# Local attention's two pairs multiplied with V in one step on four row groups, and V of the strided classes loaded in two transfers a batch

## The chip, the cores and the metric

The kernel runs on one core of one Trainium2 chip. Its five engines work at the same time, each through its own list of instructions in order: TensorE (PE; its weight loads are shown as PEld) multiplies matrices into PSUM, VectorE (DVE), ScalarE (ACT) and GpSimd (POOL) work on elements, SyncE (SP) issues the DMAs, which run on 16 DMA engines. The metric is the device time of one execution in microseconds.

## The reference

Eight batches, eight heads, 576 positions, 64 numbers a head. Heads 0 to 3 see the last 32 positions (local), heads 4 to 7 the earlier positions of the same class modulo 32 (strided, 18 positions a class). The attention's output, 512 wide, goes through a gated layer.

```python
mask_local = (rel >= 0) & (rel < stride)          # stride = 32
mask_strided = (rel >= 0) & (pos[None, :] % stride == pos[:, None] % stride)
scores = np.where(masks[None], scores, -1000000000.0)   # scores = q k^T / sqrt(64)
attn = softmax(scores)
x = (attn @ v) as [batch, seq, 512]
...
gate_pre += conv_w[k][None, None, :] * xp[:, k:k + S, :]   # 5 taps, causal
gate = 1.0 / (1.0 + np.exp(-gate_pre))
out = (gate * (x @ w_val)) @ w_out
```

## The kernel before

The program works on one batch after the other and keeps everything with channels on the 128 partitions, x transposed. A batch has these steps; the letters name them in the whole text.

- L (three a batch): local scores of two pairs of heads, 24 matmuls of 64 x 64 from `qLs` and `KL` into two banks of PSUM; mask by DVE, softmax by DVE, POOL and ACT, then a transpose into `PL`.
- Y (two a batch before): the weights in `PL` times V in `vLs`. `vLs` holds, on the 32 partitions 64a + 32p, half a of the sequence of pair p. One Y takes one pair p: ten key windows, two heads, two halves, 40 matmuls on two row groups (32 partitions each) into two banks. ACT copies each bank into `xs`.
- S (two a batch): strided scores, 32 matmuls from `qSs` and `KBS` into one bank; softmax; transpose into `PT`, copied into a block diagonal `BDS`.
- T (two a batch, each in two halves of 8 matmuls): `vSs` times `BDS` into one bank a half, copied into `xs`.
- X: each 128 channels of `xs` split into a high and a low part (`xhi`, `xlo`). G: the convolution and the gate; one of 32 runs as matmuls on TensorE (the "convolution" of the text, batch 0), the others on DVE.
- V: x times w_val, 12 matmuls of 384 columns for 128 channels, times the gate on DVE, split again (`ghi`, `glo`). P: times w_out, 12 matmuls of 512 columns, copied by ACT into `osb` and stored. V and P run over 12 blocks of 384 rows that go across the batches: 48 V and 36 P.

Every fp32 matmul (L, Y, S, T, convolution) shows in the trace as two passes, each with a weight load; V and P matmuls are one pass each. So one Y of 40 matmuls is 80 rows of the trace.

All q, k and v tiles exist once. A batch's load into `qSs` and `KBS` (four transfers, 1152 KB) must wait until both S steps of the batch before have read them, one into `qLs` and `KL` (1152 KB) for the last L, one into `vLs` (608 KB) for Y and one into `vSs` (576 KB) for T. Transfers stand in one queue, SP's, in a fixed order, and every one also waits for the eighth before it.

What sets the order: each step is put down with `plan.add` (engine, estimated time, group, calls). `Plan.issue` (L133 to L234) then plays the steps on a model of the engines and lets each engine take, of the steps that are ready, the one whose group stands lowest in the list `RANK`; `plan.bank()` gives a step a free bank of the six. Only the order that comes out is in the program. Where the model sees TensorE wait before 75 us, it puts in filler matmuls on a tile `idle` (L351 in the trace, L353 after the change). The trace shows every other step at L226, so steps are told apart by their tiles.

`PAIRS` (L707) says which pairs go into one Y (L532 to L546), `PVL` is the estimate for it, `load` (L301) the estimate for a transfer, `load_v` (L465) issues the loads of V. The layout of `vS` in DRAM is [batch, 4 groups, 18, 8, 256]; group g goes to partitions 32g to 32g + 31, its positions 0 to 15 to every second of them, positions 16 and 17 to two odd ones.

Of the kernel before, what the change touches and what calls it, by code (L numbers as in the profile page):

```python
# [19 lines left out]
NT = 18  # L20
# [3 lines left out]
P = 128  # L24
# [9 lines left out]
class Bank:  # L34
# [12 lines left out]
    def now(self):  # L47
        ap = self.hold["tile"]
        for name, a, k in self.chain:
            ap = getattr(ap, name)(*a, **k)  # L50
        return ap
# [6 lines left out]
class Plan:  # L58
# [11 lines left out]
    ENGINES = ("pe", "dve", "act", "pool", "sp")  # L70
    WINDOW, QUIET, BUSY, SLOW = 3.413, 0.48, 0.85, 1.9

    BLOCK, FETCH = 256, 2.4
    ISSUE, TO_DATA, TO_END = 0.6, 1.2, 0.65

    def __init__(self):
        self.filler, self.banks, self.holds = None, None, []
# [160 lines left out]
def tile_sparse_attention_moe(  # L238
# [13 lines left out]
    nc = tc.nc  # L252
# [6 lines left out]
    plan = Plan()  # L259

    def tiles(n, shape, name, dtype=F32, space=None):
        return [(space or pool).tile(shape, dtype, name=f"{name}{i}") for i in range(n)]
# [10 lines left out]
    def size(ap):  # L273
        n = 1
        for _, k in list(now(ap).ap)[1:]:
            n *= k
        return n
# [17 lines left out]
    def pe(group, took, calls, early=None, part=0):  # L295
        plan.add("pe", took, group, calls, early=early, part=part)

    def mm(out, lhsT, rhs, first=True, last=True):
        return (T.matmul, dict(out=out, lhsT=lhsT, rhs=rhs, start=first, stop=last))

    def load(group, out, in_):  # L301
        n = out.ap[0][1] * size(out)
        plan.add("sp", max(n * 4 / 320e3 + (0.25 if group[-1] == "0" or "w" in group else 0.08), 0.45), group, [(nc.sync.dma_start, dict(out=out, in_=in_))])


    ident = pool.tile([P, P], F32, name="ident")
# [12 lines left out]
    vSs = pool.tile([P, 8, 256], F32, name="vSs")  # L319
# [11 lines left out]
    gates = tiles(4, [P, 2 * S], "gate")  # L331
    BDS = Ring(tiles(NB, [P, 16, 4, NT], "BDS"))
    PS = Ring(tiles(1, [P, 32, 32], "PS"))
# [84 lines left out]
    def weight_part(name, src, dst, e, raw, t, u):  # L418
        raw = raw.rearrange("p (c f) -> p c f", c=4).bitcast(U32)
        load("load " + name, raw, src.bitcast(U32)[:, 2 * P * e:2 * P * (e + 1)].rearrange("(c p) f -> p c f", p=P))  # L420
        cols = slice(P * e, P * (e + 1))
        from_f64("make " + name, raw.rearrange("p c (f w) -> p (c f) w", w=2), t, u, dst[0][:, :, cols], dst[1][:, :, cols])
# [30 lines left out]
    def load_qk(b, kind):  # L453
        group = f"load q{kind}{b}"
        if kind == "L":
            load(group, qLs[:, :, :], qL[b])
            load(group, KL[:, :, STRIDE:], kL[b])
            return

        for j in range(2):  # L460
            load(group, qSs[j::2, :2 * S], qS[b, 64 * j:64 * j + 64])
        for j in range(2):
            load(group, KBS[j::2, j, :, :], kS[b, 64 * j:64 * j + 64])

    def load_v(b, kind):  # L465
        group = f"load v{kind}{b}"
        if kind == "L":

            for a in range(2):
                for p in range(2):  # L470
                    at = slice(64 * a + 32 * p, 64 * a + 32 * p + 32)
                    load(group, vLs[at, 1 - a:], vL[b].rearrange("(w r) f -> r w f", r=32)[:, 8 * a:9 * a + 9, 2 * D * p:2 * D * p + 2 * D])
        else:
            for g in range(4):
                load(group, vSs[32 * g:32 * g + 32:2], vS[b, g, 0:16])
            for g in range(4):
                load(group, vSs[32 * g + 1:32 * g + 32:16], vS[b, g, 16:NT])

    def attend_local(b):
        xs = xss[b % 2]  # L480
# [50 lines left out]

        for ps in PAIRS:  # L532
            group = f"Y{b}.{ps[0]}"
            banks = {(a, p): plan.bank()[:, :HALF] for p in ps for a in range(2)}
            calls = []
            for w in (1, 3, 5, 7, 9, 0, 2, 4, 6, 8):
                for h in range(2):
                    for (a, p), xp in banks.items():
                        rows = slice(64 * a + 32 * p, 64 * a + 32 * p + 32)
                        rhs, q0, n = seen(rows, h, w)  # L540
                        calls.append(mm(xp[64 * h:64 * h + 64, q0:q0 + n], vLs[rows, w, D * h:D * h + D], rhs, w == 1, w == 8))
            pe(group, PVL, calls, early=0.15)
            for p in ps:
# [137 lines left out]
    for b in range(B):  # L681
        load_qk(b, "L")
        load_v(b, "L")
        load_qk(b, "S")
        load_v(b, "S")
        attend_local(b)
        attend_strided(b)
        if b == 0:

            raw = [osb2.rearrange("p i f -> p (i f)"), raws[2], raws[3], osb2.rearrange("p i f -> p (i f)")]  # L690
            for e in range(4):
                weight_part(f"wo{e}", w_out, wo, e, raw[e], *[gates[2 * i + e % 2][:, S:S + DM] for i in range(2)])
            zero("dve", "zero xs1", xss[1][:, :, 0:PADK])
        gate(b)
        for k in ((3 * b // 2,) if b % 2 == 0 else (3 * (b // 2) + 1, 3 * (b // 2) + 2)):
            value(k)
            project(k)
    names = list(dict.fromkeys(s[2] for s in plan.steps))
    tile_sparse_attention_moe.end = plan.issue(dict(zip(names, RANK)))


NB = 1
NPL = 1
TAKEN = set()
WIDE = set()
WIDES = set()
PAIRS = ((0,), (1,))  # L707
PVL = 1.5
CONV = {(0, 0)}
HELD = set()  # L710
RANK = [
# [12 lines left out]
]  # L724


# [39 lines left out]
```

## Time and profile before

| | |
|---|---|
| runs | 331.25, 336.55, 336.93 us; median 336.55 |
| the profiled execution | 331.2 us, span 329.4 us |
| granted TensorE clock, mean | 0.978 |
| TensorE busy | 311.0 us of the span (94%) |
| DVE, ACT, POOL busy | 225.4, 189.8, 180.8 us |
| moved by the DMA queues | 42.98 MB |

A row of the timeline gives the start and the length of a stretch of equal instructions in microseconds, then engine, line, operation, output and inputs, count, and in brackets how long the engine stood idle before it and for what. "issue" is idle time for which the profile shows no cause. Matmuls overlap, so a step's time is read from its start to the start of the step behind it.

### The profile page before, as it was taken

Reading aid. Unit: us, or ns where it says so; the run is one execution under the profiler, and the core shown is the slowest. Engines: PE = TensorE matmul, PEld = TensorE weight load, DVE = VectorE, ACT = ScalarE, POOL = GpSimd, SP = SyncE. Lnnn points to the kernel's source line nnn. Section 1 sums busy time; section 2 is a strip of 40 time slices with the busy share of each in tenths; the row PEclk is TensorE's granted clock in tenths of the full one; section 3 lists DMA queues with packets and bytes.
Section 4 is the critical chain, followed back from the end, with each engine's and each line's share of the span. In section 5 each row is a group of like instructions: output and inputs, shape, how many; then the busy total and the mean of one; then the engine's idle time right before and its main releaser. Section 6 shows DMA issues by size and latency. Waiting matters only on the chain.

```text
span 329.4 us, 11806 instructions
## 1 busy us (share of the span) xinstructions
PE 311.0 (94%) x5113; PEld 261.2 (79%) x5120; DVE 225.4 (68%) x438; ACT 189.8 (58%) x373; POOL 180.8 (55%) x213
## 2 busy tenths in 40 slices
PE   8986999997999999899999998999999989999995
PEld 3545567787889989688998887988998978999884
DVE  4479399997988989698592288876776951764300
ACT  4036675695578746574753294498369748442421
POOL 9664767978653964674384276556067722502610
PEclk9997699999999999999999999999999998999999
DMA  7999944469314452676302476036202200100022
GB/s 236 252 178 329 271 137 154 148 203 258 107 66 146 149 211 100 207 235 176 105 2 84 142 197 211 2 105 175 73 1 66 103 4 32 66 32 32 34 96 96
DMA packets 27267, 42.98 MB, mean 130 GB/s; under 512 B 3088, under 2 KB 16912, under 8 KB 26640
## 3 DMA queue, kind: packets, MB, share of 16 engines
q1 hardware_dynamic: 27216, 42.24, 42.9%
q8 instruction: 40, 0.66, 0.9%
q14 instruction: 11, 0.09, 0.1%
HBM read 32.79 MB, written 9.44 MB: 128 GB/s over the span
## 4 chain that ended last, share of the span: by engine, by line
PE 82%; DMA 10%; issue 3%; SPq 2%; ACT 0%; DVE 0%
PE bank L226 73%; PE bank L351 9%; DMA qSs<-in_qS_dram 6%; DMA vSs<-in_vS_dram 3%; SPq L226 2%; DMA vLs<-in_vL_dram 1%; ACT osb L226 0%; DVE idle L350 0%; DVE none L354 0%
## 5 line engine op out<-in xcount | busy, mean ns | idle before, releaser
L226 DVE SCALAR_TENSOR_TENSOR taps<-xs,cw,taps 128x576 f32<-128x576 f32 x124 | 100.6, 811 | 14.3 <-ACT taps L226 12.5
L226 PE MATMUL bank<-xhi,wv 128*128 128x384 f32 x384 | 99.7, 340 | 0.0
L226 PE MATMUL bank<-wo,ghi 128*128 128x512 f32 x288 | 90.8, 397 | 0.0
L226 POOL TENSOR_TENSOR glo<-GV,ghi 128x384 fp32r<-128x384 f32 x48 | 48.3, 1013 | 63.4 <-ACT ghi L226 62.1
L226 PEld LDWEIGHTS bank<-xhi,wv 128*128 128x128 f32 x384 | 68.8, 188 | 2.2
L226 PE MATMUL bank<-xlo,wv 128*128 128x384 f32 x192 | 64.5, 336 | 0.0
L226 PEld LDWEIGHTS bank<-wo,ghi 128*128 128x128 f32 x288 | 53.6, 190 | 11.2
L226 POOL TENSOR_TENSOR xlo<-xs,xhi 128x576 fp32r<-128x576 f32 x32 | 46.2, 1451 | 19.9 <-ACT xhi L226 19.8
L226 PE MATMUL bank<-wo,glo 128*128 128x512 f32 x144 | 56.5, 393 | 0.0
L226 DVE SCALAR_TENSOR_TENSOR GV<-gate,bank 128x384 f32<-128x384 f32 x48 | 26.0, 547 | 34.1 <-PE bank L226 18.0
L226 ACT ACTIVATE osb<-bank 128x512 f32<-128x512 f32 x36 | 21.2, 596 | 30.0 <-PE bank L226 24.5
L226 ACT COPY xs<-bank 128x288 f32<-128x288 f32 x64 | 32.0, 548 | 8.3 <-PE bank L226 8.1
L226 ACT CAST ghi<-GV 128x384 fp32r<-128x384 f32 x48 | 24.0, 510 | 21.6 <-DVE GV L226 21.4
L226 PEld LDWEIGHTS bank<-xlo,wv 128*128 128x128 f32 x192 | 36.0, 188 | 0.0
L351 PE MATMUL bank<-idle 128*128 128x512 bf16 x117 | 30.5, 411 | 5.2 <-issue 3.8
L226 ACT ACTIVATE gate<-taps 128x576 f32<-128x576 f32 x31 | 20.4, 658 | 24.7 <-DVE taps L226 24.6
L226 ACT COPY BDS<-PT 32x288 f32<-32x288 f32 x64 | 27.7, 433 | 9.7 <-DVE PT L226 8.9
L226 PEld LDWEIGHTS bank<-wo,glo 128*128 128x128 f32 x144 | 27.2, 189 | 5.9
L226 POOL TENSOR_TENSOR SML<-SML,ST 128x384 f32<-128x384 f32 x24 | 20.3, 845 | 19.0 <-DVE ST L226 18.8
L351 PEld LDWEIGHTS <-idle 128*128 128x128 bf16 x124 | 12.2, 103 | 20.6 <-issue 7.8
L226 DVE TENSOR_REDUCE ST<-SML 128x6 f32<-128x384 f32 (+1 forms) x48 | 26.0, 545 | 0.9 <-ACT SML L226 0.5
L226 PEld LDWEIGHTS bank<-PL,vLs 32*64 32x64 f32 x1280 | 21.9, 143 | 5.8 <-issue 3.4
(69 smaller groups left out, 371.1 us busy)
## 6 DMA issues: line engine op xcount, KB each, us to landing
out_dram<-osb SPq DMA_DIRECT2D x36, 256.0 KB
qSs<-in_qS_dram SPq DMA_DIRECT2D x16, 288.0 KB
qLs<-in_qL_dram SPq DMA_DIRECT2D x8, 576.0 KB
KL<-in_kL_dram SPq DMA_DIRECT2D x8, 576.0 KB
KBS<-in_kS_dram SPq DMA_DIRECT2D x16, 288.0 KB
vSs<-in_vS_dram SPq DMA_DIRECT2D x32, 128.0 KB
vLs<-in_vL_dram SPq DMA_DIRECT2D x16, 160.0 KB
vLs<-in_vL_dram SPq DMA_DIRECT2D x16, 144.0 KB
```

The lines of the kernel that those rows point to most:

```text
L226: got = [fn(**{k: now(x) for k, x in kw.items()}) for fn, kw in calls]
L351: plan.filler = lambda at: T.matmul(out=at, lhsT=idle[:, :P], rhs=idle[:, :], start=True, stop=True)
```

## The change

Both pairs' Y become one step: `PAIRS` is one tuple, so four banks are taken, and the inner loop goes over the four (a, p), four row groups in turn. The order of the sums in each bank stays. The eight loads of `vSs` become two, one for positions 0 to 15 of all four groups (64 partitions, 512 KB), one for positions 16 and 17 (8 partitions, 64 KB). The model's figures for transfers, for instruction packets and for Y are set anew, and `RANK` is another list, so all steps stand in another order.

```diff
-    BLOCK, FETCH = 256, 2.4
-    ISSUE, TO_DATA, TO_END = 0.6, 1.2, 0.65
+    BLOCK, FETCH = 256, 3.0
+    ISSUE, TO_DATA, TO_END = 0.6, 1.2, 1.2
...
     def load(group, out, in_):
-        n = out.ap[0][1] * size(out)
-        plan.add("sp", max(n * 4 / 320e3 + (0.25 if group[-1] == "0" or "w" in group else 0.08), 0.45), group, [(nc.sync.dma_start, dict(out=out, in_=in_))])
+        n = 1
+        for k in out.shape:
+            n *= k
+        plan.add("sp", max(n * 4 / 320e3 + LOAD, 0.45), group, [(nc.sync.dma_start, dict(out=out, in_=in_))])
...
-            for g in range(4):
-                load(group, vSs[32 * g:32 * g + 32:2], vS[b, g, 0:16])
-            for g in range(4):
-                load(group, vSs[32 * g + 1:32 * g + 32:16], vS[b, g, 16:NT])
+            for rows, keys in ((slice(0, P, 2), slice(0, 16)), (slice(1, P, 16), slice(16, NT))):
+                load(group, vSs[rows].rearrange("r n f -> r (n f)"),
+                     vS[b, :, keys].rearrange("g t n f -> g t (n f)"))
...
+LOAD = 0.2
-PAIRS = ((0,), (1,))
-PVL = 1.5
+PAIRS = ((0, 1),)
+PVL = 2.2
 RANK = [
-    223, 130, 85, 82, 100, 54, 253, 247, 56, 131, 268, 93, 53, 134, 241, 140, 277, 144, 154, 271, 136, 147, 195, 58,
+    101, 80, 2, 172, 13, 120, 96, 98, 5, 148, 41, 250, 4, 267, 110, 231, 29, 182, 86, 130, 26, 55, 68, 52,
...
```

TensorE at the Y of batch 1 before: the last V matmuls ahead of it and the first of Y (`PL` and `vLs`); the two banks alternate for the first 40 matmuls, then two others do.

```order
L226 MATMUL bank_114<-xhi,wv_85 128x384
L226 MATMUL bank_114<-xhi,wv_86 128x384
L226 MATMUL bank_114<-xlo,wv_85 128x384
L226 MATMUL bank_116<-PL_101,vLs 64x64
L226 MATMUL bank_115<-PL_101,vLs 64x64
```

TensorE at the Y of batch 2 after the change, behind a V as well.

```order
L226 MATMUL bank_116<-xhi,wv_85 128x384
L226 MATMUL bank_116<-xhi,wv_86 128x384
L226 MATMUL bank_116<-xlo,wv_85 128x384
L226 MATMUL bank_113<-PL_101,vLs 64x64
L226 MATMUL bank_117<-PL_101,vLs 64x64
L226 MATMUL bank_115<-PL_101,vLs 64x64
L226 MATMUL bank_114<-PL_101,vLs 64x64
```

Four banks take turns, and the 80 matmuls stand in one run; before they stood in two runs of 40, mostly with other steps between.

SP at the start, before: weights (`w_val`, `w_out`), then q and k, with the loads of `vSs` between.

```order
L226 DMA xs_77<-in_w_val_dram 128x4x256
L226 DMA qSs<-in_qS_dram 64x1152
L226 DMA osb_110<-in_w_out_dram 128x4x256
L226 DMA qLs<-in_qL_dram 128x1152
L226 DMA KL<-in_kL_dram 128x2x576
L226 DMA vSs<-in_vS_dram 16x2048 x2
L226 DMA KBS<-in_kS_dram 64x1152 x2
L226 DMA qSs<-in_qS_dram 64x1152
L226 DMA vSs<-in_vS_dram 16x2048 x2
```

SP after the change, from the sixth transfer of the program to the first load of `vSs`; ahead of it stand two pieces of w_val, conv_w, half of qSs and qLs.

```order
L226 DMA KL<-in_kL_dram 128x2x576
L226 DMA KBS<-in_kS_dram 64x1152
L226 DMA vLs<-in_vL_dram 32x9x128
L226 DMA KBS<-in_kS_dram 64x1152
L226 DMA vLs<-in_vL_dram 32x9x128
L226 DMA vLs<-in_vL_dram 32x10x128 x2
L226 DMA xs_78<-in_w_val_dram 128x4x256
L226 DMA qSs<-in_qS_dram 64x1152
L226 DMA xs_77<-in_w_val_dram 128x4x256
L226 DMA xs_78<-in_w_out_dram 128x4x256
L226 DMA osb_110<-in_w_out_dram 128x4x256
L226 DMA vSs<-in_vS_dram 64x1x2048
```

The second half of qSs went behind all of k, vLs and a third piece of w_val, and the load of vSs behind all of these.

SP after the change where batches 2 and 3 are loaded, for the places where a load of vSs stands between those that S and L wait for.

```order
L226 DMA qSs<-in_qS_dram 64x1152
L226 DMA KBS<-in_kS_dram 64x1152 x2
L226 DMA vSs<-in_vS_dram 64x1x2048
L226 DMA qSs<-in_qS_dram 64x1152
L226 DMA qLs<-in_qL_dram 128x1152
L226 DMA KL<-in_kL_dram 128x2x576
L226 DMA vSs<-in_vS_dram 8x1x2048
```

Before, the same place had four loads of 16x2048 ahead of the first half of qSs and four of 2x2048 ahead of the second.

22 rows, old and new, of the table RANK are left out of this document.

## Prediction

> **What bounds the kernel now.** I read the page first, then the chain of waits, then TensorE's timeline with its idle times. The page:
>
> ```profile
> PE 311.0 (94%) x5113; PEld 261.2 (79%) x5120; DVE 225.4 (68%) x438; ACT 189.8 (58%) x373; POOL 180.8 (55%) x213
> PE   8986999997999999899999998999999989999995
> DMA  7999944469314452676302476036202200100022
> GB/s 236 252 178 329 271 137 154 148 203 258 107 66 146 149 211 100 207 235 176 105 2 84 142 197 211 2 105 175 73 1 66 103 4 32 66 32 32 34 96 96
> q1 hardware_dynamic: 27216, 42.24, 42.9%
> q8 instruction: 40, 0.66, 0.9%
> L351 PE MATMUL bank<-idle 128*128 128x512 bf16 x117 | 30.5, 411 | 5.2 <-issue 3.8
> ```
>
> TensorE is busy 94% of the span and no other engine above 68%. But 117 of its matmuls are fillers (`idle`), 30.5 us, and they stand almost all ahead of the first V step, while the DMA queues run at nine tenths. So there are two stages: up to the first V the kernel waits for loads and for what softmax makes of them; after that TensorE's own work sets the time. The ends of the stages in TensorE's timeline (start, us, operation; idle before it in brackets):
>
> ```profile
> 13.88 1.72 PE L226 MATMUL bank<-KL,qLs 64*32 64x64 f32 x144
> 19.52 0.29 PE L226 MATMUL bank<-KBS,qSs 128*32 128x36 f32 x9
> 20.83 1.26 PE L226 MATMUL bank<-KBS,qSs 128*32 128x36 f32 x119 [1.02 <-issue]
> 27.58 0.82 PE L351 MATMUL bank<-idle 128*128 128x512 bf16 x3 [3.44 <-issue]
> 36.60 3.08 PE L226 MATMUL bank<-xs,gate 128*128 128x288 f32 x8
> 43.37 0.72 PE L226 MATMUL bank<-KL,qLs 64*32 64x64 f32 x48
> 55.83 0.70 PE L226 MATMUL bank<-xhi,wv 128*128 128x384 f32 x2
> ...
> 325.34 0.39 PE L226 MATMUL bank<-wo,glo 128*128 128x512 f32 x1
> ```
>
> The first V starts at 55.8, the last matmul ends at 325.7: 55.8 us and 269.9 us, then 3.7 us to the span's end (329.4) and 1.8 us around it (331.2). In the second stage TensorE stood still only here:
>
> ```profile
> 66.44 0.33 PE L226 MATMUL bank<-KBS,qSs 128*32 128x36 f32 x15 [1.27 <-issue]
> 77.00 1.33 PE L226 MATMUL bank<-KBS,qSs 128*32 128x36 f32 x128 [1.96 <-DMA qSs<-in_qS_dram]
> 138.94 1.33 PE L226 MATMUL bank<-KBS,qSs 128*32 128x36 f32 x128 [1.40 <-DMA qSs<-in_qS_dram]
> 195.63 1.39 PE L226 MATMUL bank<-PL,vLs 32*64 32x64 f32 x78 [0.23 <-DMA vLs<-in_vL_dram]
> 199.35 0.31 PE L226 MATMUL bank<-KL,qLs 64*32 64x64 f32 x7 [1.24 <-issue]
> 224.07 0.46 PE L226 MATMUL bank<-PL,vLs 32*64 32x64 f32 x15 [0.34 <-issue]
> 269.94 0.27 PE L226 MATMUL bank<-PL,vLs 32*64 32x64 f32 x2 [1.00 <-issue]
> 270.39 1.97 PE L226 MATMUL bank<-BDS,vSs 128*64 128x72 f32 x32 [0.18 <-issue]
> ```
>
> Loads 1.96 + 1.40 + 0.23 = 3.6 us, "issue" 4.0 us, together 7.6 us. The "issue" waits all fall in or behind long runs of small matmuls: queue q8 brings 40 packets for some 10,233 matmuls and weight loads (5113 + 5120), 256 instructions each, and a run that goes through them too fast waits for the next packet.
>
> **The Y step in one.** Before, a pair's Y runs 80 passes:
>
> ```profile
> 91.67 0.77 PE L226 MATMUL bank<-KBS,qSs 128*32 128x36 f32 x64
> 92.38 0.74 PE L226 MATMUL bank<-wo,ghi 128*128 128x512 f32 x2
> ...
> 98.08 1.39 PE L226 MATMUL bank<-PL,vLs 32*64 32x64 f32 x80
> 99.41 1.22 PE L226 MATMUL bank<-BDS,vSs 128*64 128x72 f32 x32
> 100.56 0.73 PE L226 MATMUL bank<-KL,qLs 64*32 64x64 f32 x48
> 101.21 0.62 PE L226 MATMUL bank<-xhi,wv 128*128 128x384 f32 x2
> ...
> 103.50 1.39 PE L226 MATMUL bank<-PL,vLs 32*64 32x64 f32 x80
> ```
>
> ```profile
> L226 ACT COPY xs<-bank 128x288 f32<-128x288 f32 x64 | 32.0, 548 | 8.3 <-PE bank L226 8.1
> ```
>
> From the start of one step to the next: Y 1.33 us (two pairs 2.66), T 1.15, L 0.65, V 2.3 with its switch, S 0.71. No row shows four row groups in Y. Bounds for its 160 passes: no more overlap than now, 2.66; the densest stream of the trace, S with 0.71/64 = 11.1 ns a pass, 1.78. L moves 64 columns like Y and takes 0.65/48 = 13.6 ns: 2.2 us. I take 2.2 as the nearest row, a gain of 0.46 us a batch. More than 2.66 I exclude, since the four go to four different banks. Four banks of six are taken at once and cleared by four ACT copies (548 ns each, 2.2 us); a V and a P behind them need two banks, and cover that. If the cover goes, the copies cost up to 2.2 us a batch, which stands in the upper part of the range.
>
> **What the new order does ahead of the first V.** There it now runs nine L steps, not six, and Y of two batches, not one: 3 x 0.65 + 2.66 = 4.6 us of work comes forward into waiting time, and 100 fillers stand there instead of 124. When the first V starts, I follow by the loads. L of batch 0 needs 2484 KB of the SP queue, before 2464: 13.9 as now. S needs the second half of qSs, now behind 4468 KB, before 3584: 884 KB more at about 0.24 MB/us (the first two slices), 3.7 us, so 23.2; the 32 fillers ahead of it, 30.5/117 = 0.26 us each from L's end at 15.6, hold it to 23.9. S 1.4 us, a wait for instructions as now (1.0 to 3.4; I take 2.8), Y 2.2: about 30. The L of batch 1 behind it needs q and k that lie behind 7156 KB: 7.33 MB at 0.24 is 30.5, 32 with landing, if the load of vSs ahead of them is spread evenly. I take 35 (next part). Then two L 1.3, the convolution 6.1 (now 36.60 to 43.37, less one L), L 0.7, half a T 0.6: 43.7. The S of batch 1 waits some 2.3 us for its second half; S 1.4, T 0.6, 11 fillers 2.9, T 1.15, 2 fillers 0.5, three L 2.0, Y 2.2, two waits for instructions 2.3: the first V at 59.0, 3.2 us later than now (54 to 62).
>
> **vSs in two loads.** Four of the eight loads cost the SP queue 2.50 us, and the first load of an S turn is issued at once when the S step of the batch before has ended:
>
> ```profile
> 51.82 2.50 SPq L226 DMA_DIRECT2D vSs<-in_vS_dram  x4
> 68.68 0.51 SPq L226 DMA_DIRECT2D qSs<-in_qS_dram  x1
> ```
>
> Six issues fewer are 6 x 0.63 = 3.8 us of SP a batch. That is on no path of TensorE: it never waited for a vSs load longer than the trace shows above. What changes is how the bytes lie on the sixteen queues. 42.24 MB in 42.9% of 329.4 us is 299 GB/s, 18.7 GB/s a queue. 512 KB over all sixteen take 1.75 us; over four, 7.0 us, and every load issued behind it lands 5.3 us later. No row shows a load of this form: those of before took 16 rows from one run, this one takes 64 rows out of four runs of 16. I choose the four queues, since four is the one count that both the runs and the rows can be dealt by; both ends stay in the range. The Trainium skill says so: in "DMA: Bandwidth & Descriptors", section "Why a DMA increments its semaphore by 16 and not by 1", a DMA uses the largest number of engines up to 16 that divides the slowest dimension of both sides, here 64 and 4; by that rule the sum below holds, by an even spread rival 1 does. No run here shows it yet.
>
> Whom it meets: the S step of batch 2 ended at 68.58 (the V behind it starts there) and the next S could start at 77.00, a turn of 8.4 us for 1152 KB. With the vSs load between them, 13.7.
>
> ```profile
> 68.58 0.61 PE L226 MATMUL bank<-xhi,wv 128*128 128x384 f32 x2
> 317.41 0.61 PE L226 MATMUL bank<-wo,ghi 128*128 128x512 f32 x2
> ...
> 320.13 0.61 PE L226 MATMUL bank<-wo,ghi 128*128 128x512 f32 x2
> ```
>
> A P takes 2.72 us. In the new order stand between one batch's last S and the next one's first: with V at 2.2 in a row: for batch 2 a half T, 13 fillers, T, three L, Y and V, 11.5 us; for batch 3 Y, four V and P, 13.7; for batch 4 T, three V and P, 10.5; later ones 16 and more. So waits of 2.2, 0 and 3.2 us. Batch 7's L loads stand right behind a vSs load that is issued some 3 us before them; of the 5.3 I count another 2: 7.4 us.
>
> **The sum of the second stage.** 269.9; three L gone forward, -2.0; before, seven batches' Y at 2.66, now six at 2.2, -5.4; the old waits -7.6; new waits for loads +7.4; new waits for instructions +2.2 (a Y of 320 instructions in 2.2 us passes one packet's edge; edges less than 3 us apart are left at three places; the old ones came to 4.0): 264.5. With 59.0 ahead and 5.5 behind: 329.0 us against the profiled 331.2, -0.7%.
>
> That execution is like the fastest of the runs (331.25); the other two lie at 336.6 and 336.9, the median at 336.55, 1.6% above it. The trace shows nothing of why, and it may befall the new kernel as well. I say 330 for its median.
>
> **Rivals.** (1) The load is spread evenly. Then the first V stays at 55.8, the load waits shrink to 0.5: 55.8 + 257.6 + 5.5 = 319. 55.8 + 257.6 is 269.9 - 2.0 - 5.4 - 7.6 + 0.5 + 2.2 behind the old start. For it: six issues fewer a batch; against: the four runs. Chance 0.27. (2) Slower: the four queues are slow. At the mean of the first seven slices (222 GB/s, 13.9 a queue) the load takes 9.4 us, 7.1 more than spread. Two such loads ahead of the first V: +3.6. The turn is 15.5: S of batches 2 to 4 wait 4.0, 1.8 and 5.0, +5.4; L of batch 7 waits the whole 7.1, +5.1: 329.0 + 14.1 = 343.1. It decides from a load of about 8 us on. For it: DMA at 9 of 10 all through the start. Against: after 130 us the queues are half idle. Chance 0.18. (3) The change does not do what it says: Y gains nothing from four groups (+0.46 x 6 = 2.8) or loses it to the banks: 332 to 335. Chance 0.10. My forecast keeps 0.45.
>
> **The numbers.** 330; the range from (1) to (2), 319 to 343, leaves a tenth out on each side. A measurement of this kernel tells about 2% from no change. Faster by more: most of (1) and the lower edge of mine, 0.34. Slower by more: most of (2), 0.04 of mine and (3): 0.20. Within: 0.46.
>
> **What would show it.** A Y of 160 passes lasting 2.2 us (1.78 to 2.66) to the next step's start; the first V near 59; waits for qSs or KBS ahead of S of batches 2 and 4; "issue" waits of 2 to 3 us behind the first V. If the DMA share runs at nine tenths while GB/s stays up, and no S waits, rival 1 holds; a first V beyond 62, or waits of 5 us for loads in the later batches, rival 2. I would be wrong altogether if DVE (68%) or ACT became what V and P wait for under the new order.

## The result and the profile after

The changed kernel takes 348.9 us (median of four runs, 347.3 to 353.0); the kernel before, on the same chip, 334.1 (331.3 to 336.9). The ratio is 1.051, with a 95% interval of 1.044 to 1.058: slower. The forecast, 330, and its range, 319 to 343, were wrong. The profiled execution of the changed kernel is the slowest of the four, 353.0 us (span 351.2), so about 4 us of what follows belongs to it alone.

The page after, its lines that answer to those shown of before:

```profile
PE 308.4 (88%) x5096; PEld 258.9 (74%) x5096; DVE 229.0 (65%) x438; ACT 190.0 (54%) x373; POOL 180.7 (51%) x213
PE   8984597689799789799989894996799999999995
PEclk9996589899989999989999998999699999999999
DMA  8998836916625275317820575129300140120022
q1 hardware_dynamic: 26704, 42.23, 44.2%
```

TensorE's busy share fell from 94 to 88%, and no other engine rose to take its place. The dips in its row (slices 4 and 5, 25 and 28) have a lower granted clock in the same slices or the one behind. The same two stages as in the prediction, cut at the start of the first V and at the end of the last matmul, show where the time went. A row gives the stretch, its length, then busy time and instructions of TensorE, its weight loads, DVE, ACT and POOL, then the granted clock, the DMA share and GB/s. Before:

```profile
0.00:55.83 55.83, 48.98 (x904) 28.97 (x912) 37.97 (x85) 26.83 (x54) 37.14 (x55) 0.91 0.87 226
55.83:325.73 269.90, 262.03 (x4211) 232.24 (x4209) 187.41 (x354) 162.37 (x319) 143.67 (x159) 0.99 0.35 112
```

After:

```profile
0.00:64.68 64.68, 49.66 (x1193) 31.03 (x1193) 51.10 (x114) 32.52 (x65) 46.33 (x67) 0.85 0.83 221
64.68:347.46 282.78, 258.70 (x3908) 227.89 (x3904) 177.89 (x324) 156.89 (x307) 134.39 (x147) 0.97 0.37 100
```

The first stage is 8.9 us longer, all but 0.7 of it idle. In the second TensorE has less to do (258.7 against 262.0), but stands still for 24.1 us instead of 7.9. The larger waits, and one Y with the V behind it, in TensorE's timeline after:

```profile
29.64 0.35 PE L226 MATMUL bank<-KBS,qSs 128*32 128x36 f32 x8 [4.87 <-issue]
40.44 0.45 PE L226 MATMUL bank<-KL,qLs 64*32 64x64 f32 x10 [2.85 <-issue]
63.25 1.49 PE L226 MATMUL bank<-PL,vLs 32*64 32x32 f32 x79 [2.28 <-issue]
...
69.33 0.76 PE L226 MATMUL bank<-KBS,qSs 128*32 128x36 f32 x64 [1.56 <-DMA qSs<-in_qS_dram]
82.91 2.09 PE L226 MATMUL bank<-PL,vLs 32*64 32x64 f32 x160
84.92 0.61 PE L226 MATMUL bank<-xhi,wv 128*128 128x384 f32 x2
97.44 1.19 PE L226 MATMUL bank<-KBS,qSs 128*32 128x36 f32 x64 [3.23 <-DMA qSs<-in_qS_dram]
118.92 0.76 PE L226 MATMUL bank<-KBS,qSs 128*32 128x36 f32 x64 [1.95 <-DMA qSs<-in_qS_dram]
147.90 0.95 PE L226 MATMUL bank<-BDS,vSs 128*64 128x72 f32 x16 [1.75 <-ACT osb L226]
177.25 1.22 PE L226 MATMUL bank<-BDS,vSs 128*64 128x72 f32 x32 [1.35 <-DMA vSs<-in_vS_dram]
216.09 0.83 PE L226 MATMUL bank<-KL,qLs 64*32 64x64 f32 x48 [4.59 <-DMA KL<-in_kL_dram]
247.73 1.63 PE L226 MATMUL bank<-KL,qLs 64*32 64x64 f32 x96 [4.67 <-DMA KL<-in_kL_dram]
```

The chain of waits says what these loads stood behind (start, us, what):

```profile
56.63 12.57 DMA qSs<-in_qS_dram
85.34 12.01 DMA qSs<-in_qS_dram
131.40 10.51 DMA out_dram<-osb
196.01 12.40 DMA vSs<-in_vS_dram
208.43 7.53 DMA KL<-in_kL_dram
238.91 10.01 DMA out_dram<-osb
```

The load of vSs issued at 196.01 lands 12.4 us later. Every transfer waits for the eighth before it, and the eighth behind that load, which is for batch 6, is KL of the same batch: SP cannot issue it before 208.43, it lands at 216.0, and L of batch 6 starts at 216.09. L of batch 7 (247.73) waits for a KL that was issued at 235.04, 3.4 us behind a vSs load (231.67). The halves of qSs issued at 56.63 and 85.34, 0.7 and 5.3 us behind a vSs load of 512 KB (at 55.94 and 80.02), take 12 us, and S waits for them (69.33 and 97.44). And two output stores take 10 us: they go through the same queues, `osb` has room for two, so ACT can't clear a P's bank until a store has landed. Both kinds of wait, as SP's own queue and ACT show them after (us, times, longest):

```profile
SPq L226 <- DMA vSs<-in_vS_dram: 23.1, 5, 6.9
...
ACT osb L226 <- DMA out_dram<-osb: 22.6, 6, 6.3
```

Before, SP waited 1.6 us for vSs and ACT 5.3 us for stores.

A wait is also dearer than its length. The stretch around the wait that ends at 247.73, after:

```profile
238.00:243.00 5.00, 5.00 (x174) 3.97 (x172) 4.26 (x10) 3.39 (x8) 3.17 (x5) 1.00 1.02 219
243.00:248.00 5.00, 0.33 (x25) 0.30 (x32) 0.46 (x1) 0.00 (x0) 0.82 (x1) 0.92 0.73 146
248.00:251.40 3.40, 3.17 (x100) 2.60 (x84) 2.69 (x6) 2.44 (x6) 0.74 (x1) 0.50 0.45 144
251.40:255.00 3.60, 3.60 (x12) 2.86 (x11) 2.47 (x7) 3.36 (x7) 2.93 (x4) 0.63 0.14 53
```

Behind 4.67 us of idle time the granted clock is 0.50 for some 6 us, and the P there takes 4.93 us (249.59 to 254.52) instead of the 2.72 of the prediction's row. The Trainium skill has this in "TensorE: Matmul & The Clock Gate", section "HAM oscillation — how this bites in real kernels": gaps of more than about 3.4 us bring the half clock back. The trace agrees for this wait, but gives no such limit: behind the 3.23 us that end at 97.44 the clock is 0.50 as well (to 99.00), behind the 1.75 us that end at 147.90 it is 0.58 (to 150.00), and behind the 1.95 us that end at 118.92 it stays at 1.00. From what length on a wait slows the clock, these runs don't show.

### The profile page after: what moved, and what is told of

Read it like the earlier page. It is cut to its first block, busy times and chain, and to the rows that moved or that the text cites. A ratio compares the mean times of both kernels' runs of the same rounds, so it can differ in the third digit from the quotient of the medians.

```text
span 351.2 us, 11718 instructions
## 1 busy us (share of the span) xinstructions
PE 308.4 (88%) x5096; PEld 258.9 (74%) x5096; DVE 229.0 (65%) x438; ACT 190.0 (54%) x373; POOL 180.7 (51%) x213
## 4 chain that ended last, share of the span: by engine, by line
PE 61%; DMA 31%; issue 2%; ACT 2%; SPq 1%; DVE 1%; ACTq 0%
PE bank L226 56%; DMA qSs<-in_qS_dram 10%; DMA KL<-in_kL_dram 8%; DMA vSs<-in_vS_dram 7%; DMA out_dram<-osb 7%; PE bank L353 5%; SPq L226 1%; ACT osb L226 1%; ACT BDS L226 0%; DVE taps L226 0%; DVE ST L226 0%; ACT gate L226 0%; DVE SML L226 0%; ACT ghi L226 0%; DVE SMS L226 0%
## 5 line engine op out<-in xcount | busy, mean ns | idle before, releaser
L226 PE MATMUL bank<-wo,ghi 128*128 128x512 f32 x288 | 94.8, 411 | 0.2 <-ACT osb L226 0.2
L226 PEld LDWEIGHTS bank<-wo,ghi 128*128 128x128 f32 x288 | 56.1, 199 | 12.6 <-ACT osb L226 0.5
L226 PE MATMUL bank<-wo,glo 128*128 128x512 f32 x144 | 58.2, 404 | 0.0
L226 PEld LDWEIGHTS bank<-wo,glo 128*128 128x128 f32 x144 | 28.2, 196 | 6.4
L226 PE MATMUL bank<-KL,qLs 64*32 64x64 f32 x1152 | 17.5, 239 | 15.8 <-DMA KL<-in_kL_dram 10.6
L226 PEld LDWEIGHTS bank<-KL,qLs 64*32 64x32 f32 x1152 | 14.2, 112 | 21.2 <-issue 19.2
L226 POOL TENSOR_TENSOR PB<-SML,ST 128x384 f32<-128x384 f32 x24 | 20.8, 866 | 12.5 <-DVE ST L226 8.2
```

Source lines behind the costliest of these rows:

```text
L226: got = [fn(**{k: now(x) for k, x in kw.items()}) for fn, kw in calls]
```

## The experiments

A run is a block of rows that lie one behind the other in DRAM without a gap. Theory A: the form of the load. Its source has four runs, so it is dealt onto four of the sixteen DMA engines (the prediction calls them queues), and what is issued behind it waits. Theory B: the new order itself starves TensorE. Theory C: the Y step on four banks costs time.

**One run instead of four (even).** V of the strided classes is laid out so that the 64 rows are one run; TensorE's order is the changed kernel's, row for row.

```diff
-                load(group, vSs[rows].rearrange("r n f -> r (n f)"),
-                     vS[b, :, keys].rearrange("g t n f -> g t (n f)"))
+            load(group, vSs[0:P:2].rearrange("r n f -> r (n f)"), vSa[b])
+            load(group, vSs[1:P:16].rearrange("r n f -> r (n f)"), vSb[b])
...
+        "vSa": vs[:, :, :16].reshape(B, 64, 8 * 4 * D),
+        "vSb": vs[:, :, 16:].reshape(B, 8, 8 * 4 * D),
```

> The changed kernel with one thing altered: V of the strided classes lies in DRAM so that positions 0 to 15 of all four groups are 64 rows in one run (and positions 16 and 17 another array of 8 rows). The same two transfers a batch, of the same bytes, at the same places of the same order; TensorE's order is the same row for row. Theory A (the form of the load: a source of four runs is dealt onto four of the sixteen DMA queues, and every load and every store issued behind it waits for those four): the DMA-ended idle times of 1.5 to 4.7 us in the second stage go, the first V comes at 56 to 60 instead of 64.7, and the time falls from 348.9 by 18 to 28 us, to 321 to 331. Theory B (the new order itself starves TensorE, whatever the form): 343 to 349, the first V at 63 or later. Theory C (the Y step on four banks, or the clock, costs the time): no change, 346 to 350.

317.18 us, 0.953 of the kernel before (0.948 to 0.958): 31.7 us below the changed kernel, and faster than both. The two stages with one run:

```profile
0.00:58.96 58.96, 49.64 (x1192) 30.69 (x1192) 49.51 (x109) 30.29 (x61) 44.44 (x65) 0.89 0.81 254
58.96:311.67 252.71, 250.91 (x3908) 222.34 (x3904) 179.65 (x330) 158.56 (x311) 136.40 (x149) 1.00 0.33 110
```

Against the changed kernel's profile the first stage is 5.7 us shorter and the second 30.1: 22.3 us of idle time gone (24.1 to 1.8), and 7.8 us less for the same 3908 matmuls, at a clock of 1.00 instead of 0.97. An output store lands in 2.0 us (median), where two took 10. Theory A holds, B and C fall as causes of the loss. The fall was larger than the 18 to 28 us expected; the 7.8 us of the clock had no place in that figure.

**Eight transfers in the new order (eight), the new form in the old order (narrow).** The first issues the four loads of 128 KB, and the four of 16 KB, one behind the other where the change has its two. The second is the kernel before with the changed load, at the place of the first of the four that it replaces:

```diff
-            for g in range(4):
-                load(group, vSs[32 * g:32 * g + 32:2], vS[b, g, 0:16])
...
+                    whole = [(nc.sync.dma_start, dict(out=vSs[first:P:step].rearrange("r n f -> r (n f)"),
+                                                      in_=vS[b, :, keys].rearrange("g t n f -> g t (n f)")))]
```

> The changed kernel, with V of the strided classes again in eight transfers a batch (four of 128 KB and four of 16 KB, as before the change), the four of each issued one behind the other where the changed order has its two; everything else in the same order. Theory A (form of the load): as with the even spread, 321 to 333, since each of these transfers comes from one run; the 3.8 us more that SP needs a batch is at most some us on the path. Theory B (order): 343 to 349. If it stays 5 us or more behind the version with two even transfers, the number of issues matters too.

> The kernel before, with only the load of the strided V in the new form: two transfers a batch, the source in four runs, each issued where the first of its four stood; all other engines in the old order row for row, Y still in two steps. Theory A (form of the load): it loses most of what the change lost, 342 to 350 against 334 to 337, with DMA-ended waits of 3 us and more ahead of S or T and the first V 2 to 8 us later. Theory B (order): 331 to 337, like the kernel before. In between, both parts weigh.

321.09 us (0.964, 0.957 to 0.971) and 351.16 us (1.050, 1.038 to 1.062). The form alone makes the old order as slow as the changed kernel (1 us above the 342 to 350 expected); with the old form the new order is faster than the old. In the narrow version SP waited 17.9 us for vSs, where it had waited 1.6. The two-transfer version with one run is 3.9 us ahead of eight transfers, less than the 5 us set beforehand as the sign that the number of issues matters.

**Two transfers with one run in the old order (old_even).** Y in two steps, as before.

> The kernel before, its order unchanged on all other engines, Y in two steps, with the strided V in two transfers a batch whose source is one run (64 rows and 8 rows), each at the place of the first of the four it replaces. It gives what the number of transfers is worth alone, with an even spread: against the kernel before (332.8 in the last comparison) 0 to 5 us faster, 328 to 333, since TensorE waited for loads 3.6 us in all there. If the whole gain of the version with one run came from the loads and none from the order and Y, it is 317 to 322.

331.34 us, ratio 1.000 (0.995 to 1.004). Six issues fewer a batch are worth nothing in the old order, and the gain of the version with one run (14 us, 331.3 to 317.2) comes with the new order and Y.

**Y pair after pair (seq, even_seq).** Within the one step, pair 0's 40 matmuls and then pair 1's, first in the changed kernel, then in the version with one run:

```diff
+            calls = calls if len(ps) == 1 else [c for p in ps for i, c in enumerate(calls) if i % 4 // 2 == p]
             pe(group, PVL, calls, early=0.15)
```

> The changed kernel with Y's 80 matmuls in the order of pair 0's 40, then pair 1's 40, still in one step with four banks: two row groups in turn, not four. If four row groups overlap as the trace says (1.86 to 2.01 us a step against 2 x 1.33 before), each Y here takes about 2.6 us and the time is 0 to 5 us longer than the changed kernel's 348.9 (0 where the loads' waits hide it, 4.5 where none is hidden). Theory C (the step with four banks in turn costs time): it is faster than the changed kernel, below 346.

> The version with 64 rows in one run (317.2 us), with Y's 80 matmuls as pair 0's 40 and then pair 1's 40, two row groups in turn. In the changed kernel this cost nothing (348.7 against 348.9). If that is because the waits for loads hid it, then here, where TensorE hardly waits, it shows: seven Y of 0.65 us more, 3 to 6 us longer, 320 to 323. If Y on four row groups gains nothing by itself: 316 to 318.5.

348.70 us, like the changed kernel. With one run 322.75 us against 317.18: 5.6 us. So the gain is there; with the narrow load the waits hide it (in seq those for KL are 3.83 and 3.86 us instead of 4.59 and 4.67). In the two profiled executions the six Y behind the first V take 14.8 us against 11.3, 3.5 more, and the first V comes 1.9 later (60.88). The Y behind 76 us, with pairs in turn and with one run a load:

```profile
76.76 2.60 PE L226 MATMUL bank<-PL,vLs 32*64 32x64 f32 x160
79.29 0.62 PE L226 MATMUL bank<-xhi,wv 128*128 128x384 f32 x2
```

2.53 us, against 2.00 at the same place with four groups in turn and one run (74.35 to 76.35), and 2.01 in the changed kernel (82.91 to 84.92). Theory C falls: four row groups in turn gain.

**Two and eight runs (runs2, runs8).** The source of the 64 rows in two runs of 32 or eight of 8, a spare row behind each:

```diff
+            load(group, vSs[0:P:2].rearrange("r n f -> r (n f)"), vSa[b, :, 0:32])
+        "vSa": _np.pad(vs[:, :, :16].reshape(B, 2, 32, 8 * 4 * D), ((0, 0), (0, 0), (0, 1), (0, 0))),
```

> The version whose 64 rows lay in one run, with the rows of positions 0 to 15 now laid out in DRAM as two runs of 32, a spare row behind each; nothing else differs from it (317.2 us) and the order is that of the changed kernel (four runs: 348.9). Theory A (as many queues as divide the number of runs and of rows): two queues, each load takes twice as long as with four (the changed kernel's took about 12 us), every load and store behind it waits, and SP stands still for the load to land: 385 to 450. Rival (the cost is that the source isn't one run, whatever the number of runs): 345 to 355, as with four.

> The same with eight runs of eight rows, a spare row behind each. Theory A: eight queues, a load takes some 3.5 us more than over sixteen at most: 319 to 328, far nearer to one run (317.2) than to four (348.9). Rival (any source of several runs is slow): 345 to 355. Rival (more runs are worse): above 349.

374.47 us with two runs (1.131 of before, 1.116 to 1.146), 325.66 with eight (0.982, 0.967 to 0.996). The order of the four forms is theory A's, and the rivals fall; but two runs cost less than the 385 expected. In the changed kernel the load of 64 KB comes from four runs too, in these two kernels from one, so what lies between four runs and two or eight is not the large load's alone. The same load of batch 6 from issue to landing, in the chain of waits with two runs:

```profile
214.89 15.01 DMA vSs<-in_vSa_dram
```

and with eight:

```profile
181.25 8.65 DMA vSs<-in_vSa_dram
```

So 15.0 us with two, 12.4 with four, 8.65 with eight, and a median of 4.5 with one run.

**The load by itself (alone).** Behind the last store of the version with one run, five more loads of the same 512 KB, each issued when the one before has landed; they compute nothing.

```diff
+    for source in (vSa[7], v8[:, 0:8], v4[:, 0:16], v2[:, 0:32], vSa[7]):
+        nc.sync.dma_start(out=vSs[0:P:2].rearrange("r n f -> r (n f)"), in_=source)
```

> The version with one run, and behind its last output store five more loads of batch 7's 64 rows into the tile, one after the other, each issued when the one before has landed: from one run, from eight runs, from four, from two, from one run again. They compute nothing and nothing else is in flight at the second to the fifth. What a load takes by itself, from issue to issue of the next: theory A, as many queues as runs, each at 18.7 GB/s (the rate worked out from the page): about 2 us for issue and landing, plus 1.75 us from sixteen queues, 3.5 from eight, 7.0 from four, 14.0 from two: 3.8, 5.5, 9.0, 16.0, 3.8. If a queue is slower by itself (12.6 GB/s, as 12.4 us for four would say): 4.6, 7.2, 12.4, 22.8. Rival (several runs cost the same, however many): 8, 4 and 2 runs take about 10 us each.

SP's timeline at the end of this kernel: the second, third, fourth and fifth load (eight, four, two runs, one run), each start being the landing of the load before.

```profile
316.00 0.66 SPq L706 DMA_DIRECT2D vSs<-in_v_dram  x1
322.26 0.57 SPq L706 DMA_DIRECT2D vSs<-in_v_dram  x1
330.83 0.52 SPq L706 DMA_DIRECT2D vSs<-in_v_dram  x1
343.52 0.52 SPq L706 DMA_DIRECT2D vSs<-in_vSa_dram  x1
```

6.26 us from eight runs, 8.57 from four, 12.69 from two; the last one, from one run, landed 0.5 + 3.1 us after its issue began (SP's wait for it at the end: 3.1). Of theory A's 3.8, 5.5, 9.0 and 16.0 for one, eight, four and two runs the first three are near and the last is 3.3 us too long; the slower queues (4.6, 7.2, 12.4, 22.8) and the rival's equal 10 us fall. This is one execution. Here are stretches inside each load, with the DMA share in the last column but one:

```profile
319.00:321.00 2.00, 0.00 (x0) 0.00 (x0) 0.00 (x0) 0.00 (x0) 0.00 (x0) 0.50 0.48 147
326.00:329.00 3.00, 0.00 (x0) 0.00 (x0) 0.00 (x0) 0.00 (x0) 0.00 (x0) 0.50 0.24 93
334.00:341.00 7.00, 0.00 (x0) 0.00 (x0) 0.00 (x0) 0.00 (x0) 0.00 (x0) 0.50 0.13 54
345.30:346.50 1.20, 0.00 (x0) 0.00 (x0) 0.00 (x0) 0.00 (x0) 0.00 (x0) 0.50 0.86 314
```

The share is the mean over sixteen engines: 0.48, 0.24 and 0.13 are 7.7, 3.8 and 2.1 of them, the eight, four and two of the number of runs; with one run it is 0.86. That is the rule of the Trainium skill that the prediction cited, now shown by a run. The prediction's price, 5.3 us more than spread, fits this load alone (8.57 less 3.6 is 5.0), in part by luck: for two runs the same reckoning gives 12.3 us more, and the load took 9.1 more. In the kernel it is 12.4 against 4.5, 7.9 us more.

**Stores by ACT (stores_act, even_stores_act).** The 36 output stores are issued by ACT behind each copy into `osb`, first in the changed kernel, then with one run:

```diff
+            plan.steps[-1][3].append((nc.scalar.dma_start, dict(out=out[r0:r0 + P, :], in_=osb)))
```

> The changed kernel, four runs a load as there, with the 36 output stores issued by ACT right behind the copy into osb instead of by SP in its queue; the loads stay with SP in the same order. It asks through what the narrow load delays the stores (22.6 us of ACT's idle time ended on them). If by the place in SP's list (its waits for the load, and stores standing behind loads): ACT's wait for stores falls below 6 us and the time by 5 to 15 us, to 334 to 344. If by the DMA queues' own work, whoever issues: 346 to 351 and ACT's wait stays near 20 us. ACT gets 36 issues of about 0.6 us more, which could cost up to some us.

> The control of the run before it: the version with one run (317.2 us), its stores issued by ACT as well. It shows what the move costs or gives without the narrow load: 315 to 322. The effect of the move on the narrow version is to be read against this one.

344.92 us (340.7 to 348.6; ratio 1.029, 1.015 to 1.044) and 318.56 (0.954, 0.944 to 0.964). The move takes 4.0 us off the narrow version and costs the control 1.4. As ratios to the kernel before, taken anew beside these runs, it is 1.051 to 1.029 and 0.953 to 0.954. So the stores' place in SP's list was worth some 5 to 8 us; the single runs with the narrow load lie 8 us apart, so the size is rough. ACT's wait for stores, with the narrow load:

```profile
ACT osb L226 <- DMA out_dram<-osb: 10.9, 5, 4.7
```

It falls from 22.6 to 10.9, not below 6: neither expectation holds whole. Part of the stores' delay is SP's list, part stays when another engine issues. The larger rest of the 31.7 us stayed, and so did the waits for loads: SP still waited 33.0 us for vSs, and TensorE 16.3 for KL and qSs.

## Why the prediction was wrong, step by step

**The ledger.** The profiled executions differ by 353.0 less 329.0, 24.0 us: 5.7 in the first stage (64.7 against 59.0) and 18.3 in the second (282.8 against 264.5), which is 14.5 more idle time (24.1 against the 7.4 + 2.2 counted), 7.8 of matmuls at a lower clock, which was in no term, and 4.0 less work than counted (254.9 against the 250.9 that the same matmuls take at full clock).

**The step that failed is "Whom it meets".** The form was read rightly, four queues, and the price of the load by itself too. What was too small is its reach. I added 5.3 us, the price of the load by itself, to one turn of loads and charged S of batches 2 and 4 and L of batch 7, 7.4 us. The runs show three things in its place: in the kernel the load takes 12.4 us; SP, which may not run more than eight transfers ahead, stops until it has landed (23.1 us in all) and issues nothing, a limit that was known and that no term had; and the output stores stand behind it too, so that `osb`, a bank and at last TensorE wait. Of the 24.1 us of idle time, S of batches 2, 3 and 4 had 6.7 (1.56, 3.23, 1.95; forecast 2.2, 0, 3.2). That sum is near the 5.4 forecast by luck, since the longest of the three fell where none was forecast. L of batches 6 and 7 had 9.3 (4.59, 4.67; forecast 0 and 2), and this is where most is missing: batch 6 through the stop of SP, batch 7 at the place forecast, but more than twice as long. "Issue" waits had 3.2 (2.2). T had 1.35, stores 2.2 and a wait for softmax 1.3, none of which was counted.

**The clock.** The sum took each wait at its length. The waits for L of 4.6 and 4.7 us, and two of 3.23 and 1.75, were followed by matmuls at about half the clock. The trace of before had the sign of it, behind a wait of 3.44 us, and I read only the wait: the fillers at 33.62 took 3.19 us for seven, 0.46 each, where the sum had 0.26.

**The first V.** 59.0 was forecast with the narrow load, and it came at 64.68; with one run it came at 58.96, where rival 1 had put 55.8. So in these profiles the new order costs 3 us there by itself, and the load 5.7 (with Y pair after pair it is 63.0 against 60.9, with stores by ACT 62.2 against 58.5, so the load costs 2 to 6). The loads ahead of it I had nearly right (L of batch 1 at 35, measured 36.07). Longer than counted were the "issue" waits: six up to the first V, 12.5 us in all, against 5.1. With one run the same instructions waited 4.65 (2.55 and 2.10). In the new order they came to 4.3 to 4.9 in the four kernels with one run, and to 8.0 to 12.5 in the five with two, four or eight runs (12.5 here, 8.0 with Y pair after pair); with eight transfers a batch, each from one run, 6.7. So they grew with loads of several runs, but not with these alone; in the old order they didn't grow (5.4 before, 2.2 with the narrow load, 4.6 with one run). By what way a load delays instructions, and why only there, stays open.

**Y, work and the other engines.** Y took 2.01 us at 82.91, 1.86 in later batches, in the lower half of 1.78 to 2.66; its gain was right, a little small, and hidden here. Rival 3 falls. DVE and ACT did not become the bound.

**The rivals.** Rival 2, slower, had the mechanism and the sign; its load was put at 9.4 us, and took 12.4, and its sum lacked the clock and the stores, as the forecast's did. Rival 1's time, 319, is that of the version with one run, 317.2: its premise, an even spread, is what was false. That even then the time came out so near is in part luck: its first V, 55.8, is 3.2 us too early, and its second stage, 257.6, 4.9 too long (252.7).

Taken apart by the experiments (the kernel before took 332.8 to 335.4 us beside them), the change is: the new order, with Y in one step but pair after pair, 8.6 us faster (331.3 to 322.8), Y on four row groups 5.6 more (to 317.2), and the load from four runs 31.7 slower (to 348.9). The parts depend on this sequence: with the narrow load in both, new order and Y together are worth only 2 us (351.2 to 348.9).

## What to carry to other kernels

When several loads become one, look at the outermost size of both sides: with a source of four runs one transfer used four of sixteen DMA engines, and laying the source out as one run turned a loss of 5% into a gain of 5%. Price a slow transfer by all that stands behind it in the issuing queue, the stores and the limit on transfers in flight included, and not by the one reader it feeds. A TensorE wait can cost more than its length: here a wait of 4.7 us was followed by a P of 4.93 us instead of 2.72.

## What the runs showed of the hardware

- A load's time does not halve with twice the queues: alone 12.69, 8.57, 6.26 and 3.6 us for two, four, eight and sixteen. Inside these loads a busy engine moved 19 GB/s of eight, 24 of four and 26 of two (147, 93 and 54 GB/s over 7.7, 3.8 and 2.1 engines), where the prediction reckoned with 18.7 for each.
- In the kernel the same loads took 15.0, 12.4, 8.65 and 4.5 us, 0.9 to 3.8 more than alone. What shares the engines with them was not taken apart.
- Stores issued by another engine than the loads escaped half of the delay (22.6 to 10.9 us). The Trainium skill, "DMA: Bandwidth & Descriptors", section "Queues, rings and completion order", says that each DMA engine takes turns between the rows of SP and of ACT; a store would then pass the loads queued in SP's row but share the busy engines. The two numbers, of one execution each, fit that, and no run here separates it from SP's own waits.
